# Sums of value weights split by VectorE in place a step later, squares of the second batch on ScalarE, and another order of steps in the third batch and at the end

## The chip, the cores and the metric

The kernel runs on one core of a Trainium2 chip. Its time is the device time of one execution in microseconds (us), taken as the median of several runs. The engines are named as the profile names them: PE is TensorE (matrix products and transposes), with its weight loads apart as PEld; ACT is ScalarE, DVE is VectorE, POOL is GpSimd, and SP is the engine that issues all DMAs here, one after the other.

## The reference

```
B, H, Sl, Sg, D = 8, 8, 512, 32, 64      # batches, heads, local and global tokens, head size
# attention: global queries see everything, local ones the globals and a band of +-32 positions
out_g = softmax(q_g @ [k_g, k_l].T / 8) @ [v_g, v_l]
out_l = softmax([q_l @ k_g.T, banded(q_l @ k_l.T)] / 8) @ [v_g, v_l]
x = concat([out_g, out_l]) -> (8, 544, 512)
# feed-forward: each token is mixed with the one before it
xk = mu_k * x + (1 - mu_k) * x_prev ;  xr = mu_r * x + (1 - mu_r) * x_prev
k = relu(xk @ w_k)                       # w_k 512 x 1024
v = (k * k) @ w_v                        # w_v 1024 x 512
out = sigmoid(xr @ w_r) * v              # w_r 512 x 512
```

Everything is float32. The kernel writes each operand of the feed-forward products as a high part (a cast to the reduced format fp32r) and a low part (the value less the high part), and multiplies high by high, high by low and low by high.

## The kernel before, in words

**Stages.** Each of the 8 batches has an attention part, four units of two heads, and a feed-forward part for two halves of 256 tokens each (t0 and t1), made of blocks of 24 or 48 products: keys (xk times w_k), gates (xr times w_r) and values (squares times w_v). The attention of a batch runs interleaved with the feed-forward of the batch before. `in_turn` takes its steps by a string, `BATCH`: A is a step of attention, F one of the feed-forward. At each F a dictionary `todo` says which preparing work is issued beside that step: `mixing` (token mixing, whose results xkh, xkl, xrh and xrl are split into high and low), `part` (the split of one operand into bh and bl), `difference` (a sum or difference of operands).

**Two ways to make values.** Batches 0 and 1 (numbers below `FROM` = 2) use plain products, `keys_and_gate` and `values`. From batch 2 on, the values of both halves come together from seven products instead of eight, after Strassen: `values_1` makes B11, B21 and T2, `values_2` makes T3, T1, T4 and B22, each name being the operand on the right. Their left operands are sums of blocks of w_v. `sums_of_values` makes those sums beside the feed-forward of batch 1, at its steps 4 to 19: four rounds, in each two additions on POOL (L278), four more (L283 to L287), then the split into `hs` and `ls`, stored to a scratch in DRAM. They are loaded again when used (`a`).

**Order on the engines.** PE runs in program order throughout (`in_line`). From batch 1 on, ACT, DVE and POOL too run strictly in the order of the code; a waiting instruction holds everything behind it on its engine. Before that a scheduler chose the order.

**Buffers.** `stage` (tag w64) has three buffers, shared by `a`, `hs`, `ls` and staged weights. Of PSUM, three banks serve the products in turn (tag m), four the scores, and one the transposes of softmax results (tag t). So `transposes` can write the bank again only after ACT has copied it out into PT (L408); a unit has four such groups of transposes, each put between two blocks of products.

**The end.** After the last attention, `end()` runs the last batch's values and the feed-forward of all global tokens (`final`, 256 of them). K is a block of its keys, V one product of the last batch, G its gates, E its own values.

Of the kernel before, what the change touches and what calls it, by code (L numbers as in the profile page):

```python
# [10 lines left out]
F32 = mybir.dt.float32  # L11
F32R = mybir.dt.float32r
# [4 lines left out]
AF = mybir.ActivationFunctionType  # L17
# [3 lines left out]
P = 128  # L21
# [14 lines left out]
def window_of(i):  # L36
    return min(max(i - 1, 0), NW - 1)
# [19 lines left out]
TOK = 256  # L57
# [9 lines left out]
def local_global_attention_then_rwkv_ffn(  # L67
# [12 lines left out]
    nc = tc.nc  # L80
# [8 lines left out]
    stage = ctx.enter_context(tc.tile_pool(name="stage", bufs=3))  # L89
# [38 lines left out]
    line = {"on": False, "last": None, "all": False}  # L128
# [21 lines left out]
    for g, row in enumerate(ROWS):  # L150
        for r, i in enumerate(row):
            at = START[window_of(i)] // CK
            for n, c in enumerate(ORDER[at:at + 4]):
# [5 lines left out]
                else:  # L159
                    nc.gpsimd.affine_select(  # L160
                        out=m, in_=m, pattern=[[i - c, CK]], base=0, channel_multiplier=c - i,
# [94 lines left out]
    FROM = 2  # L256
    LEFT = ("A11", "A21", "A12", "A22", "S2", "S3", "S4", "S1")
    HC = NF // 2
    scratch = dramp.tile([P, len(LEFT), HC, 2, TOK], F32, name="scratch")

    def behind(store):
        tc.add_manual_dep(
            store.ins, Tokens.square.ins.name,
            mybir.DependencyInfo(mybir.DependencyClass.Sync, mybir.DependencyReason.DATA),
        )

    def sums_of_values():

        for i in range(HC):
            a = stage.tile([P, 2, 2, TOK], F32, tag="w64", name="a")  # L270
            hs, ls = (stage.tile([P, 4, TOK], F32R, tag="w64", name=f"{x}s") for x in "hl")
            for j in range(2):
                f = i + j * HC
                for x, part in enumerate((wv_h, wv_l)):
                    part = part[:, f].bitcast(F32).rearrange("p (e n) -> p e n", e=2)
                    store = nc.sync.dma_start(out=scratch[:, 2 * j:2 * j + 2, i, x], in_=part)
                    behind(store)
                nc.gpsimd.tensor_add(  # L278
                    a[:, j], *(w[:, f].bitcast(F32).rearrange("p (e n) -> p e n", e=2) for w in (wv_h, wv_l))
                )  # L280
                yield
            a11, a21, a12, a22 = (a[:, j, e] for j in range(2) for e in range(2))
            nc.gpsimd.tensor_add(a22, a21, a22)  # L283
            nc.gpsimd.tensor_sub(a21, a11, a21)
            nc.gpsimd.tensor_sub(a11, a22, a11)
            yield
            nc.gpsimd.tensor_sub(a12, a12, a11)  # L287
            s = a.rearrange("p j e n -> p (j e) n")
            nc.scalar.copy(hs, s)  # L289
            nc.vector.tensor_sub(ls, s, hs.bitcast(F32))  # L290
            for x, part in enumerate((hs, ls)):
                nc.sync.dma_start(out=scratch[:, 4:8, i, x], in_=part.bitcast(F32))
            yield

    V1 = (("A11", "B11"), ("A12", "B21"), ("S2", "T2"))
    V2 = (("S3", "T3"), ("S1", "T1"), ("A22", "T4"), ("S4", "B22"))
# [252 lines left out]
    class Tokens:  # L549
# [65 lines left out]
        def keys_and_gate(self):  # L615
            self.kk_h, self.kk_l = [], []
            for f0 in range(0, NF, 2):
                kp = psum("m").rearrange("p (j n) -> p j n", j=2)
                for j in range(2):
                    products(kp[:, j], wk_h, wk_l, slice((f0 + j) * P, (f0 + j + 1) * P),  # L620
                             lambda c: self.xk_h[:, c], lambda c: self.xk_l[:, c], NC)
                rk = self.two(tmpp, "relu")
                nc.scalar.activation(rk, kp, AF.Relu)
                k2 = self.two(tmpp, "k2")
                Tokens.square = nc.gpsimd.tensor_mul(k2, rk, rk)
                kh = self.two(mlp, "kkh", F32R, f"kkh{f0}")
                kl = self.two(mlp if f0 + 2 < NF else mlp1, "kkl", F32R, f"kkl{f0}")
                nc.scalar.activation(kh, rk, AF.Square)
                nc.vector.tensor_sub(kl, k2, kh.bitcast(F32))  # L629
                self.kk_h += [kh[:, j] for j in range(2)]  # L630
                self.kk_l += [kl[:, j] for j in range(2)]
                yield
            yield from self.gates()
# [331 lines left out]
    keys = [t.keys_and_gate() for t in first]  # L965
# [37 lines left out]
    for i, pair in enumerate(pairs_0):  # L1003
        all_transposes(R[i])
        final = transposes_global(Pg[i], fill=((0, 8), (16, 8))[i])
# [15 lines left out]
    for i, pair in enumerate(pairs_0):  # L1021
        final = all_transposes(R[2 + i])
# [33 lines left out]
    def batch(b, before):  # L1056

        nonlocal leftp, sump, gate3
        if b < FROM:
# [3 lines left out]
            todo = {  # L1063
                0: lambda: t0.mixing("k2"),
                1: lambda: t0.mixing("r0"),
                2: lambda: t0.mixing("r2"),
                8: lambda: t1.mixing("k0"),
                9: lambda: t1.mixing("k2"),
                10: lambda: t1.mixing("r0"),
                11: lambda: t1.mixing("r2"),  # L1070
                18: lambda: keys_at(FROM).tokens[0].mixing("k0"),
# [12 lines left out]
        this = keys_at(b)  # L1084
# [14 lines left out]
        def mix(t, *parts):  # L1099
            for x in parts:  # L1100
                t.mixing(x)

        def mix_next(*parts):
            mix((keys_at(b + 1) if b + 1 < B else final).tokens[0], *parts)

        if b == FROM:
            steps = chain(before.values(), this.keys(t0), gates_of(0), this.keys(t1), gates_of(1))
            todo = {
                0: lambda: mix(t0, "r0"),
                1: lambda: mix(t0, "r2"),  # L1110
                3: lambda: begin_halves(),
                7: lambda: mix(t1, "k0"),
                8: lambda: (mix(t1, "k2"), this.part("B11", 0)),
                9: lambda: (mix(t1, "r0"), this.part("B11", 1)),
                10: lambda: (mix(t1, "r2"), this.difference("T1", 0)),
                11: lambda: (this.part("B21", 0), this.difference("T1", 1)),
                12: lambda: (this.part("B21", 1), this.made("T2", 0)),
                13: lambda: (this.difference("T2", 1), mix_next("k0")),
                14: lambda: this.difference("T3", 0),
                15: lambda: mix_next("k2", "r0"),  # L1120
            }
        else:
            steps = chain(before.values_1(), this.keys(t0), gates_of(0), before.values_2(), this.keys(t1), gates_of(1))
            todo = {
                0: lambda: (before.left_over(0), mix(t0, "r2")),
                1: lambda: before.left_over(1),
                2: lambda: before.left_over(2),
                3: lambda: before.left_over(3),
                4: lambda: before.left_over(4),
                6: lambda: mix(t1, "k0"),  # L1130
                7: lambda: mix(t1, "k2"),
                8: lambda: mix(t1, "r0"),
                9: lambda: before.left_over(5),
                10: lambda: (before.left_over(6), mix(t1, "r2")),
                11: lambda: this.part("B11", 0),
                12: lambda: (this.part("B11", 1), this.part("B21", 0)),
                13: lambda: (this.part("B21", 1), this.difference("T1", 0)),
                14: lambda: this.difference("T1", 1),
                15: lambda: this.made("T2", 0),
                16: lambda: (this.difference("T2", 1), mix_next("k0")),  # L1140
                17: lambda: mix_next("k2"),
                18: lambda: (mix_next("r0"), this.difference("T3", 0)),
            }
# [9 lines left out]
    final = Keys([global_tokens()])  # L1153

    def keys_at(b):
# [3 lines left out]

    BATCH = {  # L1160
        FROM - 1: "AFAFAFAFAF" "AFFAFFF" "AFAFAFAFAF" "AFFAFFF",
        FROM: "AFAFAFAFAF" "AFFAF" "AFAFAFAFAF" "AFFAF",
        None: "AFAFAFAFAF" "AFFAFF" "AFAFAFAFAF" "AFFFAFF",
    }
    last = first[1]
# [5 lines left out]
    for b in range(1, B):  # L1171
        if b < B - 1:
# [4 lines left out]
            last = keys_at(b) if b >= FROM else batch.last  # L1177
    t, = final.tokens
    for _ in batch(B - 1, last):
        pass  # L1180
    last = keys_of[B - 1]

    def end():
        for n, _ in enumerate(last.values_1()):
            last.left_over(n)
            if n == 0:
                t.mixing("r2")
            yield
        last.left_over(3)
        last.left_over(4)  # L1190
        change_use(LAST_USE)
        keys, gates, values, ends = final.keys(t), t.gates(), last.values_2(), final.values_of_one()
        todo = {
            1: lambda: last.left_over(5),
            3: lambda: last.left_over(6),
            4: lambda: final.part("B11", 0),
            5: lambda: (final.part("B11", 1), final.part("B21", 0)),
            7: lambda: final.part("B21", 1),
        }
        for n, x in enumerate("KVKVKVKVEGEGEE"):  # L1200
            next({"K": keys, "V": values, "E": ends, "G": gates}[x], None)
            todo.get(n, lambda: None)()
            yield
    for _ in end():
        pass
# [49 lines left out]
```

## Time and profile before

| quantity | value |
|---|---|
| runs shown | 679.15, 680.05, 689.79 us, median 680.05 |
| profiled execution | 687.01 us, of which the span from first to last instruction is 685.2 |
| busy time in the span | PE 643.4, DVE 502.7, POOL 354.0, ACT 342.6 us |
| mean granted TensorE clock | 0.965 of full speed |
| DMA | 127.15 MB, 186 GB/s on average |

Busy times are shares of the one span, so they overlap. PE is busy 94% of it. What matters for a change to the order of work are the stretches in which PE isn't busy or runs at a lower clock, and what ended each. In the rows of the trace, an idle time stands in brackets ahead of the instruction that ended it, with what released that instruction.

### The profile page before, as it was taken

The page shows a single profiled execution, that of the slowest core. Times are in us where ns is not written, and L with a number is a line of the kernel's source. Part 1 is how long each engine was busy: PE and PEld are TensorE (multiplying, and loading weights), DVE is VectorE, ACT ScalarE, POOL GpSimd, SP SyncE. Part 2 cuts the span into 40 slices and gives each one's busy share as a digit, 9 for nine tenths or more (in the row PEclk, how much of TensorE's full clock was granted, in tenths as well). Part 3 has the DMA queues.
Part 4 walks back from the last instruction along what each step waited for, and adds up shares of the span by engine and source line. Part 5 has one row for each costly group of instructions (what it writes and reads, how often), then busy time and mean ns, then how long its engine had stood idle before and what let it go on. Part 6 is the DMA issues. An engine that isn't in the chain of part 4 may idle for free.

```text
span 685.2 us, 20545 instructions
## 1 busy us (share of the span) xinstructions
PE 643.4 (94%) x8362; PEld 609.8 (89%) x8362; DVE 502.7 (73%) x1296; ACT 342.6 (50%) x1066; POOL 354.0 (52%) x326
## 2 busy tenths in 40 slices
PE   6689899999689599999999999999999999999898
PEld 4568789999679589998999999999999999999898
DVE  4695977446936537987689869896989696777971
ACT  4885757626237156646455554646374624213121
POOL 6376657235745513376436653674448443652740
PEclk9977979999889899999999999999999999999999
DMA  8835515247527354182847375646746380543774
GB/s 334 322 102 193 198 64 215 85 162 264 182 78 274 109 171 184 42 300 76 287 159 263 122 263 215 220 164 216 261 183 201 110 293 5 197 150 143 232 224 159
DMA packets 43565, 127.15 MB, mean 186 GB/s; under 512 B 4048, under 2 KB 20944, under 8 KB 43472
## 3 DMA queue, kind: packets, MB, share of 16 engines
q1 hardware_dynamic: 43472, 125.85, 52.5%
q8 instruction: 66, 1.08, 0.6%
q14 instruction: 27, 0.22, 0.1%
HBM read 108.53 MB, written 17.30 MB: 184 GB/s over the span
## 4 chain that ended last, share of the span: by engine, by line
PE 79%; DVE 8%; DMA 4%; POOL 3%; issue 3%; ACT 2%; SPq 0%; POOLq 0%; DVEq 0%
PE ps_m L141 59%; PE ps_s L141 14%; PE ps_t L144 5%; DMA w<-w_k 2%; DMA raw_v<-v 2%; DVE diff L608 2%; PE ps_t L141 1%; DVE xfull L608 1%; DVE diff L603 1%; DVE B L721 1%; DVE xkh L612 1%; DVE kkl L629 1%; DMA w<-w_r 0%; ACT Pt L368 0%; ACT hs L289 0%
## 5 line engine op out<-in xcount | busy, mean ns | idle before, releaser
L141 PE MATMUL ps_m<-xkh,wk_h 128*128 128x256 f32 x544 | 157.5, 290 | 1.1 <-ACT gate L659 1.1
L141 PE MATMUL ps_m<-xkl,wk_h 128*128 128x256 f32 x544 | 153.9, 283 | 1.0 <-POOL xkl L581 1.0
L141 PE MATMUL ps_m<-xkh,wk_l 128*128 128x256 f32 x544 | 153.1, 282 | 1.4 <-issue 1.3
L141 PE MATMUL ps_m<-bh,a 128*128 128x256 f32 x736 | 136.5, 282 | 0.0
L374 POOL TENSOR_TENSOR Pt<-Pt,ssum 128x512 f32<-128x512 f32 x64 | 69.9, 1099 | 87.1 <-DVE ssum L327 51.2
L141 PEld LDWEIGHTS ps_m<-bh,a 128*128 128x128 f32 x736 | 114.8, 189 | 0.0
L141 PEld LDWEIGHTS ps_m<-xkh,wk_h 128*128 128x128 f32 x544 | 104.3, 192 | 6.8 <-issue 1.7
L141 PEld LDWEIGHTS ps_m<-xkl,wk_h 128*128 128x128 f32 x544 | 104.7, 193 | 2.4 <-POOL xkl L581 1.2
L141 PEld LDWEIGHTS ps_m<-xkh,wk_l 128*128 128x128 f32 x544 | 104.9, 193 | 1.5 <-issue 1.5
L368 ACT ACTIVATE Pt<-Pt,m 128x128 f32<-128x128 f32 x256 | 99.4, 392 | 13.6 <-DVE m L362 12.9
L141 PE MATMUL ps_m<-bl,a 128*128 128x256 f32 x368 | 102.9, 280 | 2.3 <-POOL bl L729 2.1
L644 ACT ACTIVATE relu<-ps_m 128x512 f32<-128x512 f32 x52 | 31.0, 596 | 94.4 <-PE ps_m L141 94.4
L141 PE MATMUL ps_m<-xrh,wr_h 128*128 128x256 f32 x272 | 76.8, 282 | 0.0
L141 PE MATMUL ps_m<-xrl,wr_h 128*128 128x256 f32 x272 | 75.4, 277 | 0.0
L613 POOL TENSOR_TENSOR xkl<-xfull,xkh 128x512 fp32r<-128x512 f32 x30 | 40.1, 1336 | 68.2 <-DVE ssum L326 38.5
L141 PE MATMUL ps_m<-xrh,wr_l 128*128 128x256 f32 x272 | 75.2, 277 | 0.0
L362 DVE CUSTOM_DVE_ANT_0 Pt<-ps_s,masks 128x128 f32<-128x128 f32 x256 | 55.9, 285 | 21.8 <-PE ps_s L141 21.5
L141 PEld LDWEIGHTS ps_m<-bl,a 128*128 128x128 f32 x368 | 69.2, 188 | 2.8 <-POOL bl L729 2.8
L408 ACT COPY PT<-ps_t 128x512 f32<-128x512 f32 x56 | 32.7, 583 | 66.1 <-PE ps_t L144 66.0
L613 POOL TENSOR_TENSOR xrl<-diff,xrh 128x512 fp32r<-128x512 f32 x30 | 41.0, 1366 | 46.5 <-DVE xrh L612 28.1
L141 PE MATMUL ps_s<-raw_qk 64*32 64x128 f32 (+1 forms) x2112 | 58.3, 294 | 5.6 <-DMA raw_qk<-qk 5.5
L144 PE MATMUL ps_t<-ident,Pt 128*128 128x128 f32 x256 | 40.4, 285 | 21.5 <-ACT PT L408 17.5
(126 smaller groups left out, 1549.5 us busy)
## 6 DMA issues: line engine op xcount, KB each, us to landing
a<-scratch SPq DMA_DIRECT2D x92, 512.0 KB, 4.7
raw_v<-v SPq DMA_DIRECT2D x32, 896.0 KB, 7.6
raw_qk<-qk SPq DMA_DIRECT2D x32, 624.0 KB, 5.0
out_l<-gate SPq DMA_DIRECT2D x32, 256.0 KB, 4.1
w<-w_k SPq DMA_DIRECT2D x8, 512.0 KB, 9.4
w<-w_v SPq DMA_DIRECT2D x8, 512.0 KB, 3.8
w<-w_r SPq DMA_DIRECT2D x4, 512.0 KB, 3.2
scratch<-wv_h SPq DMA_DIRECT2D x8, 256.0 KB, 4.8
```

Source lines behind the costliest of these rows:

```text
L141: return in_line(nc.tensor.matmul(*a, **kw))
L144: return in_line(nc.tensor.transpose(*a, **kw))
L362: read = nc.vector.tensor_tensor_reduce(out=Pt[:, i], in0=place(t, n, h), in1=masks[:, 2 * slots[t][1] + n], op0=ALU.add, op1=ALU.min, sca ...
L368: nc.scalar.activation(Pt[:, i], Pt[:, i], AF.Exp, bias=low_x[:, i:i + 1], scale=-1.0, accum_out=ssum[:, i:i + 1],)
L374: nc.gpsimd.tensor_mul(Pt[:, some], Pt[:, some], inv.unsqueeze(2).to_broadcast([P, 4, W]))
L408: copy(pitched(j, h, 0, 4), tp.rearrange("p (g q) -> p g q", g=4))
L603: nc.vector.tensor_sub(self.shape(d[:, j]), self.cur(c0 + j), self.prev(c0 + j))
L608: nc.vector.scalar_tensor_tensor(self.shape(xf[:, j]), self.shape(d[:, j]), mu[:, c0 + j:c0 + j + 1], self.prev(c0 + j), op0=ALU.mult, op1 ...
L612: nc.vector.tensor_copy(hi[:, both], xf)
L613: nc.gpsimd.tensor_sub(lo[:, both], xf, hi[:, both].bitcast(F32))
L629: nc.vector.tensor_sub(kl, k2, kh.bitcast(F32))
L644: nc.scalar.activation(rk, kp, AF.Relu)
```

## The change

It has four parts.

1. In `sums_of_values` the split of a round's sums moves from ACT to DVE and comes a step of the feed-forward later (`finish`). DVE casts `hs`, and then subtracts it from the sums in their own place, so there is no third buffer. On POOL the third of the four additions moves a step later, next to the fourth.
2. In batch 1, `keys_and_gate` (there `line["all"]` is set) makes the square `k2` on ACT rather than POOL, and the high part `kh` by a cast of it on DVE rather than a second square on ACT. Batch 0 is unchanged.
3. In batch 2 (`BATCH[FROM]`) one F goes from the second of the string's four pieces to the last, and two preparing steps there swap places.
4. `end()` has its products in another order, with the preparing work dealt out anew.

```diff
     def sums_of_values():
+        def finish(a, hs, i):
+            s = a.rearrange("p j e n -> p (j e) n")
+            nc.vector.tensor_copy(hs, s)
+            nc.vector.tensor_sub(s.bitcast(F32R), s, hs.bitcast(F32))
+            for x, part in enumerate((hs.bitcast(F32), s)):
+                nc.sync.dma_start(out=scratch[:, 4:8, i, x], in_=part)
+        last = None
         for i in range(HC):
             a = stage.tile([P, 2, 2, TOK], F32, tag="w64", name="a")
-            hs, ls = (stage.tile([P, 4, TOK], F32R, tag="w64", name=f"{x}s") for x in "hl")
             for j in range(2):
...
+                if j == 0 and last:
+                    finish(*last)
                 yield
             nc.gpsimd.tensor_add(a22, a21, a22)
             nc.gpsimd.tensor_sub(a21, a11, a21)
+            yield
             nc.gpsimd.tensor_sub(a11, a22, a11)
-            yield
             nc.gpsimd.tensor_sub(a12, a12, a11)
-            s = a.rearrange("p j e n -> p (j e) n")
-            nc.scalar.copy(hs, s)
-            nc.vector.tensor_sub(ls, s, hs.bitcast(F32))
-            for x, part in enumerate((hs, ls)):
-                nc.sync.dma_start(out=scratch[:, 4:8, i, x], in_=part.bitcast(F32))
-            yield
+            last = a, stage.tile([P, 4, TOK], F32R, tag="w64", name="hs"), i
+            yield
+        finish(*last)
...
                 nc.scalar.activation(rk, kp, AF.Relu)
-                Tokens.square = nc.gpsimd.tensor_mul(k2, rk, rk)
+                if line["all"]:
+                    Tokens.square = nc.scalar.activation(k2, rk, AF.Square)
+                else:
+                    Tokens.square = nc.gpsimd.tensor_mul(k2, rk, rk)
-                nc.scalar.activation(kh, rk, AF.Square)
+                if line["all"]:
+                    nc.vector.tensor_copy(kh, k2)
+                else:
+                    nc.scalar.activation(kh, rk, AF.Square)
                 nc.vector.tensor_sub(kl, k2, kh.bitcast(F32))
...
-                14: lambda: this.difference("T3", 0),
-                15: lambda: mix_next("k2", "r0"),
+                14: lambda: mix_next("k2"),
+                15: lambda: (mix_next("r0"), this.difference("T3", 0)),
...
-        FROM: "AFAFAFAFAF" "AFFAF" "AFAFAFAFAF" "AFFAF",
+        FROM: "AFAFAFAFAF" "AFAF" "AFAFAFAFAF" "AFFAFF",
...
     def end():
-        for n, _ in enumerate(last.values_1()):
-            last.left_over(n)
-            if n == 0:
-                t.mixing("r2")
-            yield
-        last.left_over(3)
-        last.left_over(4)
...
-        for n, x in enumerate("KVKVKVKVEGEGEE"):
+        for n, x in enumerate("VVKVKVKVKVVEGEGEE"):
```

On ACT, in the first half of batch 1's feed-forward, the four copies of transposes stood with a cast of `hs` between the second and the third:

```order
L661 ACTIVATE gate<-gate 128x1024
L408 COPY PT<-ps_t 128x4x128 x2
L289 CAST hs<-a 128x1024
L408 COPY PT<-ps_t 128x4x128 x2
L472 COPY PT<-ps_t 96x4x2x32
```

They now follow one another (line numbers of the changed kernel run 6 to 12 ahead):

```order
L673 ACTIVATE gate<-gate 128x1024
L414 COPY PT<-ps_t 128x4x128 x4
L478 COPY PT<-ps_t 96x4x2x32
L484 COPY PT<-ps_t 64x4x32
L629 ACTIVATE relu<-ps_m 128x512
```

The cast has left the engine. At the same place DVE, before, took the low part behind the mixing of r, with a product of gate and values ahead of it and one behind it:

```order
L612 CAST xrh<-diff 128x512
L673 TENSOR_TENSOR gate<-ps_m,gate 128x512
L608 SCALAR_TENSOR_TENSOR diff<-diff,mu_r_sb,xT 128x256 x2
L612 CAST xrh<-diff 128x512
L290 TENSOR_TENSOR ls<-a,hs 128x1024
L673 TENSOR_TENSOR gate<-ps_m,gate 128x512
L629 TENSOR_TENSOR kkl<-k_2979,kkh 128x512
```

Now the cast of `hs` stands there too, and one of `kkh` ahead of the next kkl:

```order
L618 CAST xrh<-diff 128x512
L685 TENSOR_TENSOR gate<-ps_m,gate 128x512
L614 SCALAR_TENSOR_TENSOR diff<-diff,mu_r_sb,xT 128x256 x2
L618 CAST xrh<-diff 128x512
L271 CAST hs<-a 128x1024
L272 TENSOR_TENSOR a<-a,hs 128x1024
L685 TENSOR_TENSOR gate<-ps_m,gate 128x512
L638 CAST kkh<-k_2975 128x512
L641 TENSOR_TENSOR kkl<-k_2975,kkh 128x512
```

So both instructions of the split now stand ahead of the second product of gate and values. At the end of the kernel, DVE made the operands of T4 (here over the buffers B_9105) after the high parts of T3 had begun (T is T2, B_9459 and B_9460 are T3, B_9105 is T4):

```order
L728 CAST bh<-T_9553 128x512
L721 TENSOR_TENSOR B_9460<-B_9462,B_9460 128x512
L608 SCALAR_TENSOR_TENSOR diff<-diff,mu_r_sb,xg_all 128x256 x2
L612 CAST xrh<-diff 128x512
L796 TENSOR_TENSOR sum<-ps_m,sum 128x512
L728 CAST bh<-B_9459 128x512
L721 TENSOR_TENSOR B_9105<-B_9105,T_9553 128x512
L801 TENSOR_TENSOR sum<-ps_m,sum 128x512
L728 CAST bh<-B_9460 128x512
```

Now (B_9455 and B_9456 are T3, B_9101 is T4) both differences of T4 come ahead of T3's high parts, which then follow one another:

```order
L740 CAST bh<-T_9549 128x512
L733 TENSOR_TENSOR B_9101<-B_9101,T_9549 128x512
L808 TENSOR_TENSOR sum<-ps_m,sum 128x512
L733 TENSOR_TENSOR B_9101<-B_9101,T_9549 128x512
L733 TENSOR_TENSOR B_9456<-B_9458,B_9456 128x512
L740 CAST bh<-B_9455 128x512
L740 CAST bh<-B_9456 128x512
L740 CAST bh<-B_9100 128x512
```

The mixing of r (the diff and xrh of the first piece) has gone from here to a place some products later.

More of the change, by code (lines that the diff above doesn't have):

```diff
@@ L284, in sums_of_values @@
             nc.gpsimd.tensor_sub(a21, a11, a21)
+            yield
             nc.gpsimd.tensor_sub(a11, a22, a11)
+            nc.gpsimd.tensor_sub(a12, a12, a11)
+            last = a, stage.tile([P, 4, TOK], F32R, tag="w64", name="hs"), i
             yield
-            nc.gpsimd.tensor_sub(a12, a12, a11)
-            s = a.rearrange("p j e n -> p (j e) n")
-            nc.scalar.copy(hs, s)
-            nc.vector.tensor_sub(ls, s, hs.bitcast(F32))
-            for x, part in enumerate((hs, ls)):
-                nc.sync.dma_start(out=scratch[:, 4:8, i, x], in_=part.bitcast(F32))
-            yield
+        finish(*last)
     V1 = (("A11", "B11"), ("A12", "B21"), ("S2", "T2"))
@@ L1183, in end @@
     def end():
-        for n, _ in enumerate(last.values_1()):
-            last.left_over(n)
-            if n == 0:
-                t.mixing("r2")
-            yield
-        last.left_over(3)
-        last.left_over(4)
-        change_use(LAST_USE)
[L1192 to L1199, printed above, removed]
-        for n, x in enumerate("KVKVKVKVEGEGEE"):
+        change_use(LAST_USE)
+        keys, gates = final.keys(t), t.gates()
+        values, ends = chain(last.values_1(), last.values_2()), final.values_of_one()
+        at, to = last.part, last.difference
+        todo = (
+            lambda: (at("T2", 1), to("T4", 0)),
+            lambda: (to("T4", 1), to("T3", 1), at("T3", 0)),
+            lambda: (at("T3", 1), at("T1", 0)),
+            lambda: (at("T1", 1), at("T4", 0)),
+            lambda: t.mixing("r2"),
+            lambda: (at("T4", 1), at("B22", 0)),
+            lambda: None,
+            lambda: at("B22", 1),
+            lambda: final.part("B11", 0),
+            lambda: (final.part("B11", 1), final.part("B21", 0)),
+            lambda: final.part("B21", 1),
+        )
+        for n, x in enumerate("VVKVKVKVKVVEGEGEE"):
             next({"K": keys, "V": values, "E": ends, "G": gates}[x], None)
-            todo.get(n, lambda: None)()
+            if n < len(todo):
+                todo[n]()
             yield
```

## Prediction

> **What bounds the kernel now.** First the page's busy times, in all and in 40 slices:
>
> ```profile
> PE 643.4 (94%) x8362; PEld 609.8 (89%) x8362; DVE 502.7 (73%) x1296; ACT 342.6 (50%) x1066; POOL 354.0 (52%) x326
> ...
> PE   6689899999689599999999999999999999999898
> ...
> PEclk9977979999889899999999999999999999999999
> ```
>
> PE sets the end: only where it idles or is clocked down can an order gain anything. Behind the start, both rows dip in the 11th, 12th and 14th slice (171 to 205 and 223 to 240 us). That is batch 1's feed-forward, where the sums of w_v are made. So I cut that stretch, batch 2 and the end into windows (columns: stretch, length, busy time and count of PE, PEld, DVE, ACT, POOL, granted clock, share of DMA, GB/s):
>
> ```profile
> 178.79:182.06 3.27, 3.27 (x30) 3.23 (x28) 3.20 (x7) 0.00 (x0) 2.05 (x3) 1.00 0.10 30
> 182.06:191.68 9.62, 0.16 (x2) 0.03 (x1) 5.89 (x7) 1.53 (x2) 7.33 (x8) 0.61 0.08 27
> 191.68:196.16 4.48, 4.48 (x29) 4.48 (x29) 0.63 (x1) 0.59 (x1) 2.52 (x2) 0.70 0.66 234
> 220.20:223.46 3.26, 3.26 (x30) 3.22 (x28) 3.12 (x8) 1.66 (x2) 1.68 (x2) 1.00 1.04 412
> 223.46:230.86 7.40, 0.17 (x2) 0.03 (x1) 4.23 (x5) 1.53 (x2) 5.18 (x6) 0.84 0.10 36
> 230.86:236.17 5.31, 5.31 (x28) 5.31 (x29) 2.32 (x6) 0.59 (x1) 2.38 (x2) 0.58 0.58 201
> ```
>
> The first and third row hold the same work, four transposes and 24 products; so do the fourth and sixth. PE stands for 9.62 us, then does at clock 0.70 in 4.48 us what took 3.27: 9.62 + 1.21 = 10.83 lost. The second time it is 7.40 + 2.05 = 9.45. **Both together are 20.3 us**, the largest thing that could be recovered. Who ends these waits, on PE and then on ACT:
>
> ```profile
> 191.68 1.09 PE L144 MATMUL ps_t<-ident,Pt 128*128 128x128 f32 x4 [9.46 <-ACT PT L408]
> 230.86 1.09 PE L144 MATMUL ps_t<-ident,Pt 128*128 128x128 f32 x4 [7.24 <-ACT PT L408]
> ...
> 190.01 1.05 ACT L289 CAST hs<-a 128x1024 fp32r<-128x1024 f32 x1 [13.17 <-POOL a L287]
> 190.96 0.58 ACT L408 COPY PT<-ps_t 128x512 f32<-128x512 f32 x1
> 229.19 1.05 ACT L289 CAST hs<-a 128x1024 fp32r<-128x1024 f32 x1 [7.10 <-POOL a L287]
> ```
>
> The one transpose bank was written by 179.2 us (178.79 plus four transposes); its copy on ACT needed only that, but stood behind the cast of hs, which stood 13.17 us for the sums of POOL. So ACT is idle, its order is at fault, and PE pays. What is there for the other parts:
>
> ```profile
> 281.46:284.29 2.83, 2.83 (x27) 2.83 (x25) 2.83 (x26) 1.66 (x8) 1.30 (x1) 1.00 0.00 0
> 263.07:266.34 3.27, 3.08 (x28) 2.90 (x26) 2.54 (x6) 3.24 (x12) 2.48 (x2) 1.00 0.84 346
> 294.84:298.54 3.70, 3.07 (x28) 2.90 (x26) 3.56 (x8) 3.67 (x12) 2.27 (x2) 1.00 0.89 296
> 302.10:305.57 3.47, 3.07 (x28) 2.87 (x26) 3.27 (x7) 0.59 (x1) 2.65 (x4) 1.00 0.77 242
> 305.98:310.10 4.12, 2.98 (x27) 2.79 (x25) 4.09 (x8) 1.55 (x3) 4.12 (x4) 1.00 0.81 238
> 635.17:637.89 2.72, 2.72 (x26) 2.72 (x25) 2.62 (x4) 0.59 (x1) 1.74 (x2) 1.00 0.88 265
> 637.89:641.77 3.88, 3.01 (x26) 2.81 (x25) 3.85 (x6) 0.00 (x0) 2.30 (x3) 1.00 0.94 348
> 644.49:649.17 4.68, 3.30 (x26) 2.91 (x25) 4.68 (x6) 1.23 (x2) 4.25 (x3) 1.00 0.42 121
> ```
>
> Each row is one block of 24 products. A block without a wait takes 2.83 in batch 2 (first row) and 2.72 at the end (sixth). Batch 2 loses 0.44 + 0.87 + 0.64 + 1.29 = 3.24; the end loses 1.16 + 1.96 = 3.12.
>
> **The change part by part.** *The split of the sums.* ACT loses four casts and, with them, the wait. The copies of the transposes run when PE has written the bank, so both stalls fall away unless something else is late by then. That can be DVE, which now does the casts and waits for POOL's sums itself:
>
> ```profile
> 170.64 1.22 DVE L290 TENSOR_TENSOR ls<-a,hs 128x1024 fp32r<-128x1024 f32 x1 [0.58 <-ACT hs L289]
> 175.17 2.93 DVE L603 TENSOR_TENSOR diff<-xT 128x256 f32<-128x256 f32 x2
> 183.99 0.67 DVE L673 TENSOR_TENSOR gate<-ps_m,gate 128x512 f32<-128x512 f32 x1
> 186.66 0.83 DVE L612 CAST xrh<-diff 128x512 fp32r<-128x512 f32 x1
> 188.04 1.25 POOL L613 TENSOR_TENSOR xrl<-diff,xrh 128x512 fp32r<-128x512 f32 x1
> 189.25 0.72 POOL L287 TENSOR_TENSOR a<-a 128x256 f32<-128x256 f32 x1
> 191.09 1.23 DVE L290 TENSOR_TENSOR ls<-a,hs 128x1024 fp32r<-128x1024 f32 x1 [3.59 <-ACT hs L289]
> ...
> L728 DVE CAST bh<-B 128x512 fp32r<-128x512 f32 x76 | 51.7, 700 | 0.0
> L603 DVE TENSOR_TENSOR diff<-xT 128x256 f32<-128x256 f32 x56 | 39.9, 751 | 6.6 <-ACT xT L539 3.4 <-ACT B L646 3.2
> L612 DVE CAST xkh<-xfull 128x512 fp32r<-128x512 f32 x30 | 14.5, 483 | 7.2 <-PE ps_m L141 5.8
> ```
>
> In the new order the second product of gate and values (L673) stands behind the cast and the subtraction, and it empties one of the three banks that serve the products in turn. When does PE need that bank? Without the stall it goes on at 182.06, with the same transposes and 24 products as in the first window: 3.27, to 185.3. Then come a block of keys with the last transposes, the next unit's scores and a second block of keys, before the block that takes this bank. Before, these were
>
> ```profile
> 196.16:204.57 8.41, 8.41 (x185) 8.03 (x183) 3.99 (x23) 3.88 (x13) 3.54 (x4) 1.00 0.11 35
> ```
>
> 8.41 us, so the bank is needed at **193.7**. When is it free? A cast of 1024 has no row; twice one of 512 gives 0.97 (xkh) to 1.40 (bh), and I take 1.0, the nearer kind, a cast that stands among mixing as these do. Before, xrh ended at 186.66 + 0.83 = 187.5. Ahead of it DVE now has a cast of kkh (0.48) and one of hs (1.0) more and the wait of 0.58 at 170.64 less, and its diffs meet less of POOL: about 188. POOL then has xrl and the two additions left over, 1.25 + 2 x 0.75 = 2.8, to 190.8, and DVE cast, subtraction and product, 1.0 + 1.23 + 0.67 = 2.9: **193.7**. Nothing is to spare, so PE may stand for 0 to 1 us. **I take 0.5.** The ends are 0 and 8.2 (rival B). By the same walk the first gate product of the second half comes at 221 and is needed at 228; DVE stands some 2.5 us for the last sums, with nothing behind that PE needs by then, so that place costs nothing. The stores of the sums go out 1.5 to 2 us later on SP, ahead of a load of raw_v which isn't used for some 28 us: nothing.
>
> *The squares.* The rows of the kinds that are exchanged:
>
> ```profile
> L625 POOL TENSOR_TENSOR k<-relu 128x512 f32<-128x512 f32 x16 | 17.4, 1086 | 20.1 <-ACT relu L623 19.9
> L628 ACT ACTIVATE kkh<-relu 128x512 fp32r<-128x512 f32 x16 | 10.2, 640 | 0.3
> ```
>
> Of the 16, batch 1 has 8. POOL loses 8 x 1.09 = 8.7 us of work, ACT exchanges one square for another (0.64), DVE gains eight casts of 0.48 to 0.70, 4 to 5.6 us. The chain behind a block of keys was relu, 1.09 on POOL (or 0.64 on ACT), kkl; it is relu, 0.64, 0.48, kkl: the same. It takes POOL out of DVE's waits, and I cost it at nothing for PE beside the 0.7 already counted at 182. If the cover goes, it is DVE's load, and the 4 to 5.6 us lie in the same rival.
>
> A rule of the Trainium skill speaks against it: "Advanced Engine Details and Errata", section "VectorE Performance Modes", says that VectorE's second SBUF port is shared with GpSimd, so that GpSimd instructions and VectorE's two-port ones block each other. The trace agrees in part: the two diffs above took 2.93 us beside POOL's work from 175.11. By that rule casts and POOL's additions would add up, and the term of 0.5 would be the 8.2 of rival B; by the rows they mostly overlap, and 0.5 stands.
>
> *Batch 2.* The three waits of 294 to 310 (0.87, 0.64, 1.29) come of attention steps crowded in its second half; one more F lies there now, in the last piece, as in the later batches, whose stretch shows nothing of the kind:
>
> ```profile
> 330.00:627.00 297.00, 296.79 (x3785) 289.31 (x3784) 242.51 (x569) 142.64 (x431) 153.80 (x118) 1.00 0.56 193
> ```
>
> PE idles 0.21 in 297 us. The first half gives one F up: the stretch from the scores to the first transposes of the next unit shrinks by one block of 2.83, and ACT's exponentials and POOL's divisions have that much less time. I put 0.3 to 0.8 there, so 3.2 - 0.8 = **2.4 gained**; bounds 3.2, and 0.4 if the whole block's 2.83 is missed in the first half.
>
> *The end.* The two waits are for low parts on POOL:
>
> ```profile
> 640.40 0.38 PE L141 MATMUL ps_m<-bl,a 128*128 128x256 f32 x1 [0.87 <-POOL bl L729]
> 646.03 0.38 PE L141 MATMUL ps_m<-bl,a 128*128 128x256 f32 x1 [1.26 <-POOL bl L729]
> ```
>
> The mixing of r moves behind, and a block of keys comes ahead of the second and the third of these products, so the low parts have 2.7 to 5.4 us more. **3.1 gained**; bounds 0 and 3.1, since the mixing is wanted only by the gates, seven steps behind its new place.
>
> **Sum**, against the profiled execution (687.01, span 685.2, 1.8 around it): 20.3 - 0.5 + 2.4 + 3.1 = 25.3, so 661.7. The profiled one is 6.96 above the median of 680.05, and one row is a likely place:
>
> ```profile
> 82.00:96.00 14.00, 11.96 (x78) 10.03 (x77) 11.95 (x29) 6.87 (x15) 8.28 (x7) 0.63 0.28 98
> ```
>
> 78 products at 2.83/24 = 0.118 are 9.2 us, so 5 of the 7 go there, at clock 0.63, in code that isn't changed. That this comes and goes between runs is my guess; if it is there in the median after, that is 662, inside the range. Against the median: 680.05 - 25.3 = **655**.
>
> **Rivals.** *B: DVE becomes the bound.* Its work in batch 1 grows by four casts of 1024 and eight of 512, 7.8 to 11.2 us, less the waits of 0.58 and 3.59 at the first place. If DVE and POOL excluded each other, their work up to the second gate product would add up. The row below has DVE's 18.92; less some 4.7 in which it stands for POOL (2.93 for two diffs, which take 0.75 each on average, and the like), plus 0.48 + 2 x 1.0 of casts and the product's 0.67, it is 17.3. POOL's 16.35 less a square is 15. Together 32 in 25: 7 late, and 1.21 at the lower clock. That is 8.2 at one place, 655 + 8.2 = 663, or at both, 671. For it: the row of 2.93, and 193.7 against 193.7. Against it, before:
>
> ```profile
> 168.40:193.50 25.10, 15.64 (x130) 15.46 (x129) 18.92 (x26) 8.55 (x19) 16.35 (x16) 0.81 0.53 193
> ```
>
> DVE's 18.92 and POOL's 16.35 are 35.3 in 25.1 us: they overlap by at least 10.2, with waits of DVE besides.
>
> *C: the cast wasn't what held PE.* If POOL's chain ends the wait in another way, the stalls stay and only the end and batch 2 gain: 680.05 - 5.5 = 674.6, or nothing. Against it: in both places the copy starts as the cast ends (191.06 and 190.96; pipelined), and PE 0.1 behind the copy.
>
> *D: slower.* The wait of 13.17 goes with the cast to DVE, since the sums on POOL wait for DVE's xrh, and DVE now for the sums. Behind the wait stand cast, subtraction and the product that frees a bank, 2.9, so PE would stand for that bank 13.17 + 2.9 = 16.1, and in the second half 7.10 + 2.9 = 10.0 to 16.1, with 1.21 + 2.05 at the lower clock: 29.4 to 35.5 for 20.3. Less 5.5 from batch 2 and the end, that is 680.05 + 3.6 to 9.7: 684 to 690. It begins where POOL ends the sums later than 191 and turns slower where it ends them later than some 205. Against it: POOL has lost 8.7 us, and ends them by 190.8 in the walk above.
>
> *E: batch 2 and the end give nothing*, the waits only moving: 655 + 5.5 = 660.5.
>
> **How the numbers follow.** The forecast has 0.58 (651 to 658), E 0.12, B 0.18, C 0.08, D 0.04. A measurement of this kernel tells about 2% from no change: 666.4 and 693.7. Faster by more are the forecast, E and, of B, what is late at one place only, 0.13: 0.83. Within 2% are the rest of B, C and most of D: 0.15. Slower remains with 0.02. To hold 8 in 10 the range takes the forecast, E and that part of B, with a point or two for a slow median: 650 to 667.
>
> **What would show it.** Right: no PE wait above 1 us near 182 and 212, clock 1.00 from 180 to 230, no cast of hs on ACT, four on DVE, L625's multiplication eight times on POOL, batch 2's blocks at 2.83, and the stretch from 627 some 3 us shorter. Wrong: PE behind "gate L673" near 190 (B or D), transposes still waiting for PT (C), a longer wait for Pt in batch 2's first half, or casts of 1024 above 1.4 us.

## The result, and the profile after

The changed kernel took 657.55 us (median of 4 runs, 654.99 to 658.66), the kernel before 682.43 (4 runs, 679.15 to 689.79; one of 684.81 beside the three shown above). The ratio is 0.9646, with a 95% interval of 0.9582 to 0.9709: 3.5% faster, and 2.5 us from the forecast of 655. The page of the changed kernel, with the lines that were shown of before:

```profile
PE 630.7 (96%) x8362; PEld 599.6 (91%) x8362; DVE 510.9 (78%) x1308; ACT 338.4 (52%) x1062; POOL 348.4 (53%) x318
...
PE   6789899999999989999999999999999999999998
...
PEclk9799999999999999999999999999999999999999
```

The dips of the 11th, 12th and 14th slice are gone from both rows, and behind the start the clock isn't lowered any more. Here the same two places of batch 1 in windows, transposes and 24 products each (the first two rows are the first half, the others the second):

```profile
168.80:172.06 3.26, 3.26 (x30) 3.26 (x29) 3.19 (x6) 0.59 (x1) 2.35 (x2) 1.00 0.05 19
172.06:175.24 3.18, 3.18 (x30) 3.18 (x29) 3.08 (x5) 0.59 (x1) 2.75 (x4) 1.00 0.04 13
203.61:206.79 3.18, 3.18 (x31) 3.18 (x29) 3.18 (x4) 0.59 (x1) 3.07 (x4) 1.00 0.68 249
206.79:210.06 3.27, 3.27 (x31) 3.27 (x29) 0.90 (x4) 0.59 (x1) 2.41 (x3) 1.00 0.00 0
```

The second of each pair follows the first at once: 9.62 and 7.40 us of standing are gone, and 4.48 and 5.31 have become 3.18 and 3.27.

Where did the whole difference come from? PE's order is the same up to batch 2, and the same blocks come in another order behind it. So I cut both profiles at the same points of the program: the scores in batch 1 behind which the changed code begins, the first scores of batch 2, those of batch 3, the first gates of the end stretch, and the end. Before:

```profile
0.00:126.00 126.00, 110.29 (x1434) 92.89 (x1435) 89.20 (x278) 83.69 (x268) 75.42 (x103) 0.88 0.54 196
126.00:246.11 120.11, 103.41 (x1435) 99.63 (x1435) 69.31 (x197) 54.21 (x180) 61.03 (x58) 0.93 0.48 167
246.11:313.73 67.62, 63.96 (x926) 60.74 (x925) 50.90 (x149) 39.42 (x128) 32.94 (x25) 1.00 0.51 180
313.73:599.04 285.31, 285.10 (x3875) 276.66 (x3875) 233.52 (x590) 146.76 (x464) 150.41 (x117) 1.00 0.55 192
599.04:685.20 86.16, 80.68 (x698) 79.89 (x696) 59.79 (x82) 18.48 (x28) 34.17 (x24) 1.00 0.55 181
```

After:

```profile
0.00:115.91 115.91, 99.33 (x1435) 83.62 (x1435) 89.85 (x278) 83.35 (x268) 76.15 (x103) 0.97 0.57 213
115.91:216.72 100.81, 99.91 (x1435) 96.28 (x1434) 73.42 (x209) 50.15 (x176) 54.85 (x50) 1.00 0.56 194
216.72:284.37 67.65, 63.92 (x926) 60.73 (x925) 54.49 (x150) 40.05 (x128) 32.43 (x26) 1.00 0.52 186
284.37:570.28 285.91, 285.42 (x3875) 277.00 (x3875) 233.52 (x590) 146.44 (x464) 151.02 (x117) 1.00 0.55 191
570.28:655.70 85.42, 82.14 (x698) 81.94 (x696) 59.67 (x82) 18.45 (x28) 33.93 (x24) 1.00 0.55 182
```

Of the 29.5 us between the spans, **19.3 come from batch 1**, 0.0 from batch 2, -0.6 from the batches between, 0.7 from the end, and 10.1 from the first stretch, whose instructions are the same in both. So two questions are left: what each part of the change does, and what the first stretch is.

### The profile page after: what moved, and what is told of

It is laid out like the page before. It is cut to its first block, busy times and chain, and to the rows that moved or that the text cites. A ratio compares the mean times of both kernels' runs of the same rounds, so it can differ in the third digit from the quotient of the medians.

```text
span 655.7 us, 20533 instructions
## 1 busy us (share of the span) xinstructions
PE 630.7 (96%) x8362; PEld 599.6 (91%) x8362; DVE 510.9 (78%) x1308; ACT 338.4 (52%) x1062; POOL 348.4 (53%) x318
## 3 DMA queue, kind: packets, MB, share of 16 engines
q8 instruction: 66, 1.08, 0.6%
## 4 chain that ended last, share of the span: by engine, by line
PE 78%; DVE 10%; DMA 4%; ACT 3%; POOL 2%; issue 2%; SPq 1%; DVEq 0%; ACTq 0%; POOLq 0%
PE ps_m L141 60%; PE ps_s L141 12%; PE ps_t L144 4%; DMA w<-w_k 2%; DMA w<-w_v 1%; DVE diff L614 1%; DVE xfull L582 1%; PE ps_t L141 1%; POOL wv_l L240 1%; ACT Pt L374 1%; DVE a L272 1%; DVE ps_s L230 1%; DVE ps_s L227 1%; DVE kkl L641 1%; DVE bh L740 1%
## 5 line engine op out<-in xcount | busy, mean ns | idle before, releaser
L141 PE MATMUL ps_m<-xkh,wk_h 128*128 128x256 f32 x544 | 155.6, 286 | 2.7 <-DVE gate L685 0.9
L141 PE MATMUL ps_m<-xkl,wk_h 128*128 128x256 f32 x544 | 151.6, 279 | 1.2 <-POOL xkl L587 1.2
L141 PE MATMUL ps_m<-xkh,wk_l 128*128 128x256 f32 x544 | 150.9, 278 | 0.0
L141 PEld LDWEIGHTS ps_m<-xkh,wk_h 128*128 128x128 f32 x544 | 102.2, 188 | 8.5 <-issue 2.4
L141 PEld LDWEIGHTS ps_m<-xkl,wk_h 128*128 128x128 f32 x544 | 102.5, 188 | 2.1 <-POOL xkl L587 1.4
L141 PEld LDWEIGHTS ps_m<-xkh,wk_l 128*128 128x128 f32 x544 | 102.4, 188 | 0.0
L141 PE MATMUL ps_s<-raw_qk 64*32 64x128 f32 (+1 forms) x2112 | 55.4, 287 | 5.4 <-DMA raw_qk<-qk 5.4
L741 POOL TENSOR_TENSOR bl<-B,bh 128x512 fp32r<-128x512 f32 x36 | 51.9, 1459 | 14.3 <-DVE bh L740 13.9
```

The costliest lines, as they stand in the source:

```text
L141: return in_line(nc.tensor.matmul(*a, **kw))
L741: (nc.vector if b[0] == "B" else nc.gpsimd).tensor_sub(l, val, h.bitcast(F32))
```

## The experiments

**Each part alone.** These four kernels take one part of the diff each and leave the rest as before. The first:

> Only the first part of the change: the split of the sums on DVE, in place, a step later. The other three parts as before. Theory O (ACT's order was at fault: the cast of hs stood ahead of two copies of transposes): both long PE waits in batch 1 go, 17 to 19.5 us of the 19.4 that the whole change gained there; PE waits 1 to 3 us for the second product of gate and values, since POOL still makes squares; about 664. Theory P (POOL was too slow with the sums, and its relief by the squares was what counted): PE waits 5 us or more for that product, or for kkl, at one or both places; 670 or more.

It took 662.37 us (4 runs), ratio 0.9702 (0.9638 to 0.9767). Its stretch in batch 1:

```profile
120.23:222.90 102.67, 100.07 (x1436) 96.24 (x1435) 73.17 (x198) 50.15 (x176) 62.75 (x57) 1.00 0.54 188
```

And PE's new wait in it, from the timeline:

```profile
189.90 0.39 PE L141 MATMUL ps_m<-xkh,wk_h 128*128 128x256 f32 x1 [1.95 <-DVE gate L679]
```

102.67 for 120.11: the split alone brings 17.4 of the 19.3. That is theory O with its figure, also in the wait, 1.95 us for the product of gate and values. It is this wait that the prediction saw coming; in the changed kernel it is 0.90 (shown below).

> Only the second part: batch 1's squares on ACT, their high parts by a cast on DVE. Theory O: both PE waits for the copy of PT stay, each at most 1 to 2 us shorter since a square of 1.09 less stands before the sums on POOL; 678 to 683, no change that can be told. Theory P: the waits shrink by half or more; 672 or less.

It took 679.11 us (10 runs), ratio 0.9951 (0.9912 to 0.9991). Both waits stay, the cast's a little shorter (12.01 and 6.00 for 13.17 and 7.10), and the stretch in batch 1 is 118.85 for 120.11:

```profile
186.10 1.08 PE L144 MATMUL ps_t<-ident,Pt 128*128 128x128 f32 x4 [8.30 <-ACT PT L408]
...
184.43 1.04 ACT L289 CAST hs<-a 128x1024 fp32r<-128x1024 f32 x1 [12.01 <-POOL a L287]
...
222.78 1.04 ACT L289 CAST hs<-a 128x1024 fp32r<-128x1024 f32 x1 [6.00 <-POOL a L287]
```

Theory P falls: with POOL relieved, the cast still holds the copies. Beside the split the squares are worth 102.67 - 100.81 = 1.9: 1.05 in the wait for the product of gate and values, and 0.65 in a wait of PE for POOL's Pg (at 219.36 with the split alone) that is gone in the changed kernel.

> Only the third part: one step of the feed-forward goes from the first to the second half of batch 2. By the prediction 2.4 us are gained, and the waits of 0.87, 0.64 and 1.29 in the second half go. By the trace of the changed kernel (waits of 0.5, 1.5 and 1.2 in the first half, 1.1 in the second) the waits only move: from batch 2's first scores to batch 3's first scores 67.6 us before, and 67 to 68 here. No change in the time.

It took 682.32 us (10 runs), ratio 0.9998 (0.9947 to 1.0048): no change that the runs show. In its profile PE waits for the same things in the first half as in the changed kernel, and the stretch of batch 2 is 68.90, for 67.62 before.

> Only the fourth part: the other order at the end. Both theories: the two waits for low parts of POOL (1.16 and 1.96) go. Theory E1: that is 3.1 us off the time, as predicted. Theory E2: how fast the products run at the end varies from program to program (a block of 24 in 2.72 us in the trace before, 2.83 in the changed one), and where the blocks take 2.83 from the first to the last, 2 to 2.5 us of the 3.1 are lost again. The blocks' durations tell which.

It took 680.16 us (10 runs), ratio 0.9959 (0.9917 to 1.0002). Its profiled execution took 688.77 us, the longest of the ten, so only the end is read from it. The whole end stretch up to PE's last product, and one block of it:

```profile
601.64:683.78 82.14, 82.14 (x698) 81.93 (x696) 59.18 (x81) 18.43 (x28) 33.90 (x24) 1.00 0.57 187
626.82:629.65 2.83, 2.83 (x26) 2.83 (x25) 0.98 (x2) 1.23 (x2) 0.00 (x0) 1.00 0.01 4
```

PE is busy in all of the 82.14, so both waits are gone; but in the kernel before the same stretch, waits included, is 82.93 (599.04 to 681.97), only 0.8 longer. Theory E2 holds in the profile: the blocks take 2.83 to the last. In the time a gain of up to 0.8% isn't excluded.

**Engine or place?** The split came a step later as well as on another engine. This kernel has the first part of the change alone, with the place moved and the cast left on ACT (the diff is against that part):

```diff
         def finish(a, hs, i):
             s = a.rearrange("p j e n -> p (j e) n")
-            nc.vector.tensor_copy(hs, s)
+            nc.scalar.copy(hs, s)
```

> The split of the sums a step later and in place, as in the first part of the change, but the cast of hs still on ACT; the other parts as before. The cast now stands between the third and the fourth copy of transposes in the first half of batch 1, and ahead of the first in the second half. Theory O (a cast on ACT holds the copies behind it until POOL has the sums): PE still waits for PT at both places, 5 us or more each; 672 to 688. Theory S (the later step was what counted, not the engine): both waits go as in the run with the split on DVE; 661 to 667.

It took 682.00 us (10 runs), ratio 0.9982 (0.9936 to 1.0027). ACT stands for the sums as before, and PE for ACT, 6.47 us at the first place and 7.63 at the second:

```profile
188.25 0.84 PE L144 MATMUL ps_t<-ident,Pg 128*96 128x128 f32 x3 [6.47 <-ACT PT L414]
...
186.57 1.05 ACT L271 CAST hs<-a 128x1024 fp32r<-128x1024 f32 x1 [10.18 <-POOL a L296]
...
224.15 1.05 ACT L271 CAST hs<-a 128x1024 fp32r<-128x1024 f32 x1 [7.50 <-POOL a L296]
```

So it is the engine: theory S falls, and the in-order queue that holds the copies is what counted.

**The wait that the change added.** In the changed kernel, DVE's and POOL's rows at the split, and PE behind it:

```profile
179.97 1.75 DVE L271 CAST hs<-a 128x1024 fp32r<-128x1024 f32 x1 [2.91 <-POOL a L296]
181.75 2.20 DVE L272 TENSOR_TENSOR a<-a,hs 128x1024 fp32r<-128x1024 f32 x1
183.87 0.68 DVE L685 TENSOR_TENSOR gate<-ps_m,gate 128x512 f32<-128x512 f32 x1
...
179.20 0.74 POOL L296 TENSOR_TENSOR a<-a 128x256 f32<-128x256 f32 x1
179.89 2.98 POOL L285 TENSOR_TENSOR a<-wv_h,wv_l 128x512 f32<-128x512 f32 x2
...
184.61 0.38 PE L141 MATMUL ps_m<-xkh,wk_h 128*128 128x256 f32 x1 [0.90 <-DVE gate L685]
```

POOL goes straight on to the next round's additions while DVE splits. This kernel makes the first of them wait for the subtraction (`finish.low`; the lines are shortened where `...` stands):

```diff
+                if j == 0 and last:
+                    finish(*last)
-                nc.gpsimd.tensor_add(
+                add = nc.gpsimd.tensor_add(
                     a[:, j], *(w[:, f].bitcast(F32)...)
                 )
-                if j == 0 and last:
-                    finish(*last)
+                if j == 0 and last:
+                    tc.add_manual_dep(add.ins, finish.low.ins.name, ...)
```

> The changed kernel, with the next round's first addition on POOL made to wait until DVE has split the sums of the round before. In the changed kernel the cast of hs took 1.75 and the subtraction 2.20 at 180 us, while POOL ran those additions, and PE waited 1.06 for the second product of gate and values behind them. Theory X (DVE's casts and subtractions stand while POOL works): the cast takes 0.7 and the subtraction 1.2, and that wait of PE goes; 1 us faster than the changed kernel, at most, if POOL makes nothing else late. Rival (the durations have another cause): cast and subtraction stay above 1.5, or the wait stays.

It took 660.53 us (4 runs, 657.10 to 662.91), which doesn't tell it from the changed kernel. Its trace does:

```profile
182.94 0.69 DVE L271 CAST hs<-a 128x1024 fp32r<-128x1024 f32 x1 [2.91 <-POOL a L301]
183.66 1.23 DVE L272 TENSOR_TENSOR a<-a,hs 128x1024 fp32r<-128x1024 f32 x1
184.81 0.68 DVE L690 TENSOR_TENSOR gate<-ps_m,gate 128x512 f32<-128x512 f32 x1
...
184.97 2.73 POOL L287 TENSOR_TENSOR a<-wv_h,wv_l 128x512 f32<-128x512 f32 x2 [2.06 <-DVE a L272]
```

The stretch of batch 1 in this kernel:

```profile
119.05:218.58 99.53, 99.53 (x1436) 96.13 (x1435) 72.25 (x208) 49.99 (x176) 52.56 (x49) 1.00 0.57 196
```

The cast takes 0.69 for 1.75 and the subtraction 1.23 for 2.20, with POOL silent, and PE no longer stands at all in that stretch (99.53 of 99.53 busy): theory X, 1.3 us in the profile.

**Batch 2's order beside the rest.** The changed kernel without its third part:

> The changed kernel without its third part: batch 2's order is that of before. From batch 2's first scores to batch 3's first scores it was 67.7 us with it, 67.6 in the kernel before, and 66.0 where the split alone was changed. Theory M (the part only moves the waits): 66 to 67.7 here, so 0 to 1.7 us faster than the changed kernel. By the prediction: 2.4 us slower.

It took 656.33 us (4 runs, 651.95 to 662.70); the stretch of batch 2 is 67.6. The part moves waits and shows no gain, as theory M says, and 2.4 us of loss, as by the prediction, don't appear; the runs can't tell less. Over all 14 profiles the stretch is 66.0 to 70.5 in the eight with the old order and 67.0 to 68.9 in the six with the new. One wait makes much of this spread: 5 to 10 us into the stretch PE stands for 0 to 2.6 us, with either order, and the profile names nothing that ended it. In the first pair of profiles it is 1.30 before and 0.19 after, so the equal lengths there hide that the other waits have grown by about 0.8.

**The pace of the products.** What makes the blocks at the end take 2.83 in one kernel and 2.72 in another? This kernel puts four transposes ahead of the last batch's products:

```diff
     t, = final.tokens
+    tp = psum("t")
+    for i in range(4):
+        transpose(tp[:, i * P:(i + 1) * P], ident, ident)
     for _ in batch(B - 1, last):
         pass
```

> The changed kernel, with four transposes of the identity put on PE, read by nothing, behind the last attention and ahead of the last batch's products. In the trace, blocks of 24 products take 2.83 from there to the end in the changed kernel, and 2.72 at the end of the kernel before, behind a short disturbance. Theory F (the pace of products is one of two, 113 or 118 ns, and is set anew when PE does something else or waits): some 36 blocks take 2.72 in place of 2.83, 4 us less for 0.4 of transposes, so 3 to 4 us faster than the changed kernel. Rival (something else sets the pace, such as traffic or heat): blocks stay at 2.83, and it is 0.4 slower.

Its first block behind the transposes, and the whole end:

```profile
549.28:552.00 2.72, 2.72 (x27) 2.72 (x26) 1.82 (x5) 1.51 (x2) 2.03 (x2) 1.00 0.09 11
568.42:648.20 79.78, 79.29 (x698) 78.92 (x696) 59.17 (x81) 18.45 (x28) 33.89 (x24) 1.00 0.58 192
```

Blocks of 2.83 stand right ahead of them (545 to 549), of 2.72 behind, to the last: 79.78 for 82.14, with the granted clock at 1.00 in both. In all 12 profiles without these transposes the blocks at that place take 2.83. So the transposes do change the pace. But they aren't the only thing that does: the kernel without the third part, which has the same end and no such transposes, goes over to 2.72 at 590 us, where two products start 0.36 us apart, not 0.12, and its end is as short:

```profile
574.54:654.51 79.97, 79.89 (x698) 79.52 (x696) 59.10 (x81) 18.45 (x28) 33.90 (x24) 1.00 0.57 191
```

And in the kernel before the blocks go over at 619 us with no wait and nothing else on PE (no two products there start more than 0.13 us apart). Theory F holds for the transposes; that a disturbance is needed isn't shown, and what sets the pace is open. In the time nothing shows: the profiled execution took 653.21 us, the three others 664.85 to 667.40 (mean granted clock 0.997, and 0.974 to 0.985), and why those are longer is open.

**Both additions together**, beside the changed kernel once more:

> The changed kernel once more, beside the next one on the same chip: 655 to 663. In the profiles so far the time up to the first scores of batch 1's last two units, which no part of the change touches, was 116 to 126 us; the same spread is expected here. From there to batch 2's first scores 100.8, to batch 3's 67.7, and the blocks at the end 2.83.

> The changed kernel with POOL's addition behind the split and with the four transposes at the end. By the profiles of the two apart, PE doesn't wait for the second product of gate and values (1.2 less) and the blocks at the end take 2.72 (2.6 less): 3 to 4 us faster than the changed kernel on the same chip, 652 to 660. If the pace is only a matter of chance from run to run, the blocks take 2.83 again and it is 0 to 1 faster.

The changed kernel took 660.25 us (6 runs, 654.79 to 668.42; ratio 0.9609, 0.9564 to 0.9654), and with both additions it took 658.37 (6 runs, 654.17 to 661.96; ratio 0.9605, 0.9563 to 0.9646). In the profile the stretch in batch 1 is 99.55 for 101.1, and the end 79.5 for 82.1. The time can't tell the two apart: the intervals are wider than the 4 us.

**The first stretch.** In the profiles of these kernels the first stretch, the same instructions in each, took 115.9 to 126.0 us, and the longer values were mostly in kernels with the cast on ACT. So the kernel before was profiled twice more:

> The kernel before once more, for its profile. The part up to the scores in batch 1 at 126.0 us in the first profile, the same instructions in every kernel here, took 121.5 to 126.0 in the five kernels with the cast of hs on ACT, and 115.9 to 122.8 in the seven with it on DVE. Theory C (chance from run to run): anything from 116 to 126. Theory A (something in the part itself goes with the change): 121 to 126 again. From there to batch 2's first scores 120, with the two waits for PT.

> The same kernel a third time, for the same question: by chance 116 to 126, else 121 to 126. Two values below 121 would speak for chance; two above leave it open.

```profile
0.00:115.78 115.78, 99.86 (x1434) 84.26 (x1434) 89.82 (x278) 83.28 (x268) 76.22 (x103) 0.97 0.58 213
```

The first took 115.78, the shortest of all, at clock 0.97 (680.77 us in all), the second 120.29 (681.83). So the stretch varies from execution to execution of one and the same kernel, by 10 us. Over 14 profiles its mean is 122.3 us in the seven with the cast on ACT and 119.2 in the seven with it on DVE; whether a part of these 3 us goes with the change stays open.

## Why the prediction was right, and where not

- **The two stalls, 20.3: right.** Batch 1 is 19.3 shorter in the first pair of profiles. In all three profiles of the kernel before it takes 120.1, 121.9 and 120.1, and in two of the changed one 100.8 and 101.1. Rivals C and D are out: the split alone gives 17.4, and PE stands 0.90 us, not 16, for the product that frees the bank.
- **The wait that takes their place: the place right, the term mis-sized.** I took 0.5 and it is 1.08 (a block of 3.90 for 2.82, in the row below). The walk up to the sums' end held: POOL ends them at 179.94, and PE needed the bank at 183.5 (180.71 plus a block of 2.82). With the first stretch 10.1 shorter in this profile, that is 190.0 and 193.6, where the walk had 190.8 and 193.7. So DVE had 3.6 us for the cast, subtraction and product that I put at 2.9; they took 4.6, since POOL's next additions, right behind the sums, weren't in the walk. With POOL silent they take 0.69, 1.23 and 0.68, which would have fitted: the cast of 1024 that I estimated at 1.0 takes 0.69 alone.

```profile
180.71:184.61 3.90, 3.00 (x28) 2.81 (x25) 3.87 (x4) 0.00 (x0) 3.75 (x3) 1.00 0.39 136
```

- **Rival B: its mechanism is there, its 8.2 us were not.** Beside POOL the cast takes 1.75 us for 0.69 and the subtraction 2.20 for 1.23, 2.0 us in all, and PE loses 1.08. The overlap of 10.2 us that I held against this rival doesn't speak against it: an instruction that POOL draws out is recorded as busy all the while, and so counts as overlap itself. The Trainium skill, "Advanced Engine Details and Errata", section "VectorE Performance Modes", says that GpSimd and VectorE's two-port instructions block each other. The rows of the cast agree with it.
- **The squares, at nothing: wrong by 1.9** beside the split. Without this part PE waits 1.95 for that product, not 0.90, and 0.65 for Pg, and the stretch is longer by 1.9. I said that it takes POOL out of DVE's waits, and didn't price it.
- **Batch 2, 2.4 gained: wrong, no gain shows.** I put 0.3 to 0.8 of loss for the first half, and it loses some 3.0, for 0.44 before: 0.41, 1.44 and 1.12 over the 3.27 of transposes and 24 products, in the first three of these rows. In the second half 1.1 stays of the 2.8 (the fourth row, a block of 2.83). By these waits the new order is 0.8 worse; that the stretch comes out equal goes by the wait of 1.30 early in it, which I hadn't counted and which is 0.19 after.

```profile
229.49:233.17 3.68, 3.43 (x31) 3.26 (x29) 1.21 (x3) 3.39 (x12) 0.00 (x0) 1.00 0.92 378
236.37:241.08 4.71, 3.37 (x31) 3.17 (x29) 4.61 (x9) 3.08 (x6) 2.53 (x2) 1.00 0.00 0
241.08:245.47 4.39, 3.39 (x29) 3.19 (x29) 4.18 (x9) 1.84 (x4) 2.43 (x2) 1.00 0.02 4
279.98:283.91 3.93, 2.98 (x28) 2.79 (x25) 3.93 (x4) 1.78 (x5) 3.70 (x3) 1.00 0.70 200
```

  On DVE, ahead of the wait in the second of them:

```profile
231.10 0.88 DVE L614 SCALAR_TENSOR_TENSOR xfull<-diff,mu_k_sb,xT 128x256 f32<-128x256 f32 x2 [4.58 <-ACT B L658]
...
239.38 0.16 DVE L332 TENSOR_SCALAR ssum<-ssum 128x4 f32<-128x4 f32 x1
```

  DVE stands 4.58 for a square of ACT. The division of the last Pt, for which PE waits 1.34, needs the sum in the second row, which stands behind two mixings and a split on DVE: ACT has done its exponentials by 235.8, and DVE comes to it at 239.38. I priced the lack of time for the exponentials and the divisions, not the in-order queue of DVE between them. The stated lower bound, 0.4, was just missed.
- **The end, 3.1 gained: the waits went, the sum didn't.** All 3.12 are gone, but the blocks kept the slower pace that the first of them had, and the stretch is 0.7 shorter. In the kernel without the third part, whose blocks went over to 2.72 at 590 us, the same order takes 79.97, which is 3.0 shorter: the term hangs on the pace. So rival E, which left batch 2 and the end at nothing, was nearer to what these terms did than the forecast: of 5.5 came 0.7. In the kernel before the pace had changed to 2.72 at 619 us, ahead of the two waits. The prediction compared blocks of 2.72 with waits, and didn't ask whether 2.72 would hold.
- **The sum, 25.3: so near by luck, for a reason that it didn't have.** The terms that belong to the change sum up to 19.4 in this pair of profiles, and 20.4 if the stretches behind the first are averaged over three profiles of before and two of after (557.5 and 537.1 us to PE's last product). The medians differ by 24.9 and 25.3, both times some 5 more. Where these 5 come from isn't shown: it may be the spread of the first stretch in the executions that happened to be timed, or an effect of the change on it, as the 3 us between the means of 14 profiles would have it. The guess that a dip of the clock in 82 to 96 comes and goes held: the granted clock is 0.63 there in the first profile of the kernel before and 1.00 in the second. But it is not alone: at 44 to 59 it is 0.51 and 1.00, and the whole spread is 10, not 7.
- **The signs.** Three of those named for a wrong forecast came: PE behind the second product of gate and values (0.90), a cast of 1024 above 1.4 (1.75), and a longer wait for Pt in batch 2's first half (1.34). The first two are one and the same wait, and cost 1.08; the third cost the batch 2 term.

## What to carry to other kernels

On an engine that runs in order, an instruction that waits long is paid by everything behind it: look at what stands behind the waiting instruction before asking how to make its input sooner. Moving it helps if what stands behind it on the other engine has slack, and the walk must hold the other engine's *next* work too, since it runs at the same time. Where a rearrangement shortens one half of a batch at the other's cost, price the queue that both share, not only the engine that you saw wait.

## What the runs showed of the hardware

Back-to-back products of this shape have two paces at a granted clock of 1.00: 24 take 2.72 us (113 ns each) or 2.83 (118 ns). The pace holds over long runs of equal work. Four transposes took it from 2.83 to 2.72 in two kernels of two. Short waits at the end changed it in some kernels (to 2.72 at 590 us in the one without the third part, where two products start 0.36 us apart) and not in others (it stays at 2.83 at 587.5 us in the one whose additions wait, with 0.42 us between two starts); at 619 us in the kernel before it changed with no wait at all. What sets it is open. The faster pace is worth 2.4 to 2.6 us over the last 80. And a cast of 1024 elements per partition on DVE takes 0.69 us alone but 1.75 when POOL adds at the same time.
